# Attention scores of two heads in two 64-row halves of TensorE, straight from the summed keys, in a fused attention and MoE kernel

## Chip, cores and metric

The kernel runs on one core of one Trainium2 chip. The metric is the device time of one execution in microseconds; the time of the kernel before is the median of three runs. The profile is of one further execution, whose own time and span are in the table below.

## The reference

Attention over pooled keys and values (8 batches, 8 heads, 576 queries, head size 64; 8 neighbouring keys or values are averaged, so 72 remain), then a feed-forward layer with a fixed activation:

```python
k_p = k.reshape(B, H, Sp, pool, D).mean(axis=3)
v_p = v.reshape(B, H, Sp, pool, D).mean(axis=3)
scores = scale * np.matmul(q, k_p.transpose(0, 1, 3, 2))
scores = scores - np.max(scores, axis=-1, keepdims=True)
attn = np.exp(scores)
attn = attn / (np.sum(attn, axis=-1, keepdims=True) + 1e-09)
attn_out = np.matmul(attn, v_p)
...
h = x @ w_in
sp = np.maximum(h, 0.0) + np.log1p(np.exp(-np.abs(h)))
g = h * erf(sp)
return (g @ w_out).astype(np.float32)
```

Here x is the attention's output as 4608 rows (tokens) of 512, w_in is 512 x 2048, w_out 2048 x 512.

## The kernel before

The 4608 tokens are nine chunks of 512. Chunk 0 goes through both matrix products directly, while its weights are still being brought in and split. The other eight chunks go in four pairs, and each pair's two products are done by a Strassen scheme: seven products in place of eight, on sums of weight blocks and sums of token blocks. All long products are fp32r products of 128 x 128 weights with 512 tokens, each done three times (`three`, line 742: high limb by high limb, high by low, low by high). They make up 3120 of TensorE's products and nearly all of its time.

**Attention** (`job`, line 515). A batch's pooled keys are made first. `load_pool` (line 523) brings in one pair of heads at a time, [128 rows, 72 keys, 8 neighbours], where rows 0 to 63 are the head size of one head of the pair and rows 64 to 127 that of the other, and DVE sums the 8 neighbours into the tile `ks` (line 529). Two copies on ACT (line 543) then spread `ks` over the block-diagonal tile `kbd`, [128, pair, 2 x 72]: one head's rows in the first 72 columns, the other's in the last 72, zeros elsewhere (filled once, line 426). Values are pooled in the same way into `vs`.

Queries come in tiles of 128, and one of 64 at each batch's end: 32 tiles of 128 and 8 of 64. For a tile, `scores` (line 576) does one product per pair of heads, in fp32: all 128 rows of queries as weights, 144 columns of `kbd` as the moving side, so that both heads' scores stand beside each other. Pairs 0 and 1 go into one PSUM bank, pairs 2 and 3 into another. DVE then takes the maxima (line 588), ACT the exponentials (through Sigmoid), DVE and POOL the sums and the division; TensorE transposes the result (lines 631 and 634) and multiplies it with the values (lines 674 and 675).

**Order of the work.** Nothing waits in program order by itself: `Program` (line 129) takes every operation with an engine, a cost in ns, a priority and the buffers it holds, plays the machine through eight times, and writes out the order of the shortest play for each engine. Its inputs include the number of places of each kind of buffer (`sizes`, `CAPS`, `PLACES`) and the cost that an operation is written down with (500 ns for two score products, line 583). Where the play leaves TensorE idle in the first 57 us of the planned time, it puts filler products in (`pr.filler`, line 998: a bf16 product of constants that nobody reads, into a PSUM bank kept aside for that time), which keep TensorE's clock up.

For the first pair of chunks (s = 1), `sums` (line 484) makes the weight sums on the chip: it reads raw weights back from HBM (`raw_hbm`, tile `sw`), DVE and POOL add them (lines 495 to 498), they are split into limbs (tile `ws`) and stored. `sides` (line 699) makes the sums and limbs of the tokens. `quad` (line 811) then does the seven products of one block of w_in. `head` (line 803) does one of these seven, A11 with B11, ahead of time for the first 7 of the 8 blocks, and keeps its result in the tile `p1`.

The lines of the loops over queries, and of scores before and after, are in the listing.

Of the kernel before, what the change touches and what calls it, by code (L numbers as in the profile page):

```python
# [11 lines left out]
F32 = mybir.dt.float32  # L12
# [8 lines left out]
POOL = 8  # L21
# [26 lines left out]
ON_DVE = 8  # L48
STORE = 6
HEADS = 7  # L50
EARLY, READY = (0, 0, 20, 32, 32), 14
ON_ACT = (0,)
CAPS = {"g": 32, "x": 28, "xr": 11, "w": 14, "ws": 10, "w0": 36, "gl": 12, "t": 6, "f": 3, "q": 2, "q0": 4, "f0": 14, "v": 3, "vm": 1, "low": 2, "sw": 8,
        "h": 6, "o": 4, "att": 4, "cv": 2, "dl": 3, "p1": 8}
SLACK, SLACK_SP, BIAS = 30, 400, 2000
FILL, MARGIN = 57000.0, 300
# [3 lines left out]
PLACES = 87  # L60
# [68 lines left out]
class Program:  # L129
# [100 lines left out]
    def once(self):  # L230
# [16 lines left out]
        spare = None  # L247
        if self.filler:
            spare = heapq.heappop(slots["bank"])
            self.idle.place = spare[1]  # L250
        for _ in self.ops:
# [39 lines left out]
            if spare is not None and o.eng == "PE":  # L291
                if start > FILL:
                    heapq.heappush(slots["bank"], (start, spare[1], None))
                    spare = None
                else:
                    idle = start - max(free["PE"], 3000.0) - MARGIN - (1800 if not free["PE"] else 0)
                    out.extend([self.filler] * int(idle / 107))
# [54 lines left out]
def moe_attention(ctx: ExitStack, tc: tile.TileContext, cst, qa, kl, vl, wi, wo, out):  # L352
# [13 lines left out]
    sizes = {"u": PLACES, "bank": 8, "raw": 2, "et": 1, "etb": 1, "s": 2, "m": 2, "z": 2, "bb": 1, "ks": 1, "vs": 1, "d": 5}  # L366
# [56 lines left out]
    kbd = const.tile([P, NP, 2 * SP], F32, name="kbd")  # L423
    va = const.tile([P, NP, P], F32, name="va")
    vb = const.tile([P, NP, D], F32R, name="vb")
    nc.gpsimd.memset(kbd, 0.0)
    KBD, VA, VB = (Kept() for _ in range(3))
# [85 lines left out]
    xt, made = {}, {}  # L513

    def job(ck, b, tiles, off, times, first, fresh):

        base, due, whole = times[0], times[-1] + VAL_R, ck > 2
        if fresh:
            ks, vs = buf("ks", [NP, SP]), buf("vs", [NP + 2, D])

            on_dve = b < ON_DVE

            def load_pool(src, dst, p, size, prio, tag):
                shape = [size, POOL] if on_dve else [POOL, size]
                t = buf("raw", shape) if tag == "raw" else place("v", F32, shape)
                op("SP", 15 * size, prio - 1, lambda: nc.sync.dma_start(
                    t.ap, src.rearrange("(p a b) -> p a b", p=P, b=t.ap.shape[2])), [], [t])
                if on_dve:
                    op("DVE", dve(8 * size), prio, lambda: nc.vector.tensor_reduce(  # L529
                        dst.ap[:, p, :], t.ap, AX.X, ALU.add), [t], [(dst, p)])  # L530
                else:
                    op("POOL", gps(4 * size), prio, lambda: nc.gpsimd.tensor_add(
                        t.ap[:, 0:4], t.ap[:, 0:4], t.ap[:, 4:8]), [t], [t])
                    op("POOL", gps(2 * size), prio, lambda: nc.gpsimd.tensor_add(
                        t.ap[:, 0:2], t.ap[:, 0:2], t.ap[:, 2:4]), [t], [t])
                    op("POOL", gps(size), prio, lambda: nc.gpsimd.tensor_add(
                        dst.ap[:, p, :], t.ap[:, 0], t.ap[:, 1]), [t], [(dst, p)])

            for p in range(NP):
                load_pool(kl[b, p], ks, p, SP, base + KEYS + KEYS_R * p, "raw")  # L540
            for r0, c0 in ((64, 0), (0, SP)):
                sl = slice(r0, r0 + 64)
                op("ACT", act(4 * SP), base + KEYS_S, lambda c0=c0, sl=sl: nc.scalar.copy(
                    kbd[sl, :, c0:c0 + SP], ks.ap[sl]), [ks], [(KBD, r0)])
            for p in range(NP + 2):
                load_pool(vl[b, p], vs, p, D, base + VALS + VALS_R * p,
                          "v")
# [454 lines left out]
    for o in ops:  # L1002
        o.fn()
# [37 lines left out]
```

## Time and profile before

| what | value |
|---|---|
| median of 3 runs (lowest, highest) | 871.18 us (869.67, 877.29) |
| the profiled execution | 870.09 us |
| its span, first to last instruction | 868.3 us |
| mean granted clock of TensorE | 0.996 |
| TensorE busy | 850.9 us, 98% of the span |
| VectorE (DVE) busy | 698.6 us, 80% |
| ScalarE (ACT) busy | 574.4 us, 66% |
| GpSimd (POOL) busy | 459.9 us, 53% |
| moved by DMA | 218.04 MB, 251 GB/s on average |

How to read it: the span leaves out what lies before the first and behind the last instruction. "Busy" of TensorE counts overlapping products once, and it counts fillers. PEld is TensorE's loading of weights, which runs beside its products. A product's duration holds the tail of the array's pipeline; the distance from one start to the next is what it costs in a row of products. The granted clock is 1.00 at full speed.

### The profile page before, as it was taken

What the parts mean: (1) busy time and instruction counts of PE and PEld (TensorE: products, weight loads), DVE (VectorE), ACT (ScalarE), POOL (GpSimd) and SP (SyncE); (2) the same over time, 40 slices, a digit from 0 to 9 for tenths busy, and PEclk for the clock granted to TensorE, in tenths of its full rate; (3) what the DMA queues carried; (4) which work ended last, traced back from release to release, by engine and by line L of the source; (5) the groups of instructions that cost most, each with busy time, mean ns of one, the idle gap of its engine ahead of it and who ended that gap; (6) DMA issues with size and microseconds to landing.
All of it is one profiled execution on the core that took longest, in us unless ns stands there. A gap on an engine that the chain in (4) does not pass through costs nothing.

```text
span 868.3 us, 13644 instructions
## 1 busy us (share of the span) xinstructions
PE 850.9 (98%) x4134; PEld 702.7 (81%) x4134; DVE 698.6 (80%) x1272; ACT 574.4 (66%) x989; POOL 459.9 (53%) x482
## 2 busy tenths in 40 slices
PE   8999999799999999999999999999999999999998
PEld 7787788687888888888888888887887888888886
DVE  4987898989887888688798997877879975767872
ACT  4889877569884455478985642978866446777640
POOL 2888697567786774065557352564474323442310
PEclk9999999989999999999999999999999999999999
DMA  8899999997999899885285578924753679447541
GB/s 307 312 307 342 303 402 332 324 359 266 295 316 349 331 348 311 314 317 174 85 303 160 163 257 275 362 86 134 224 152 109 219 254 340 126 131 256 190 157 50
DMA packets 125208, 218.04 MB, mean 251 GB/s; under 512 B 16976, under 2 KB 31440, under 8 KB 125136
## 3 DMA queue, kind: packets, MB, share of 16 engines
q1 hardware_dynamic: 125136, 217.18, 72.6%
q8 instruction: 33, 0.54, 0.2%
q14 instruction: 39, 0.32, 0.1%
HBM read 167.84 MB, written 49.28 MB: 250 GB/s over the span
## 4 chain that ended last, share of the span: by engine, by line
PE 72%; DVE 2%; issue 0%; ACT 0%; DVEq 0%
PE o L746 36%; PE h L746 29%; PE att L579 3%; PE att L674 3%; PE att L631 1%; PE att L675 1%; DVE g L766 0%; DVE gl L411 0%; PE att L634 0%; DVE g L894 0%; DVE g L831 0%; DVE f L918 0%; DVE ks L529 0%; DVE t L831 0%; DVE s L624 0%
## 5 line engine op out<-in xcount | busy, mean ns | idle before, releaser
L746 PE MATMUL o<-gl,w 128*128 128x512 f32 x1584 | 377.1, 393 | 0.5 <-DVE g L769 0.3
L746 PEld LDWEIGHTS o<-gl,w 128*128 128x128 f32 x1584 | 292.7, 188 | 61.9 <-DVE gl L411 0.9
L746 PE MATMUL h<-x,w 128*128 128x512 f32 x1344 | 316.9, 392 | 2.0 <-DVE t L831 1.2
L746 PEld LDWEIGHTS h<-x,w 128*128 128x128 f32 x1344 | 249.7, 188 | 55.8 <-DVE t L831 2.5
L766 POOL TENSOR_TENSOR g<-d,g 128x512 f32<-128x512 f32 x68 | 90.7, 1351 | 98.7 <-ACT d L762 75.8
L399 ACT ACTIVATE gl<-g 128x512 fp32r<-128x512 f32 x185 | 109.3, 625 | 46.2 <-DVE g L894 20.2
L411 POOL TENSOR_TENSOR gl<-g,gl 128x512 fp32r<-128x512 f32 x67 | 100.0, 1501 | 66.8 <-ACT gl L399 32.4
L411 DVE TENSOR_TENSOR gl<-g,gl 128x512 fp32r<-128x512 f32 x149 | 110.2, 767 | 6.2 <-POOL gl L400 3.9
L831 DVE TENSOR_TENSOR g<-t,h 128x512 f32<-128x512 f32 x96 | 65.5, 684 | 31.6 <-PE h L746 29.9
L758 ACT ACT_TABLE_LOAD x48 | 61.6, 1283 | 20.7 <-PE h L746 20.0
L762 ACT ACTIVATE d<-d 128x1024 f32<-128x1024 f32 x72 | 73.7, 1054 | 0.4
L894 POOL TENSOR_TENSOR g<-g 128x512 f32<-128x512 f32 x36 | 51.8, 1439 | 25.0 <-DVE g L894 19.3
L758 ACT ACTIVATE d<-g 128x512 f32<-128x512 f32 x103 | 59.1, 623 | 5.6 <-DVE g L831 5.4
L831 DVE TENSOR_TENSOR t<-t,h 128x512 f32<-128x512 f32 x57 | 39.0, 685 | 27.8 <-PE h L746 26.1
L746 PE MATMUL h<-x,ws 128*128 128x512 f32 x192 | 48.4, 407 | 4.5 <-POOL sw L496 2.9
L762 ACT ACT_TABLE_LOAD x40 | 51.3, 1283 | 0.7
L399 ACT ACTIVATE x<-xr 128x512 fp32r<-128x512 f32 (+2 forms) x60 | 32.5, 563 | 28.9 <-DVE xr L720 21.5
L746 PEld LDWEIGHTS h<-x,ws 128*128 128x128 f32 x192 | 38.0, 199 | 13.1 <-POOL sw L496 3.0
L674 PE MATMUL att<-et,va 128*128 128x256 f32 (+3 forms) x192 | 45.5, 339 | 2.0 <-DVE s L604 1.4
L579 PE MATMUL att<-kbd,q 128*128 128x144 f32 (+1 forms) x320 | 45.9, 287 | 0.4 <-DVE x L694 0.4
L579 PEld LDWEIGHTS att<-kbd,q 128*128 128x128 f32 (+1 forms) x320 | 42.3, 179 | 5.0 <-issue 1.6
L642 ACT COPY et<-att 128x512 f32<-128x512 f32 (+1 forms) x40 | 21.8, 544 | 34.5 <-PE att L631 33.5
(91 smaller groups left out, 1145.3 us busy)
## 6 DMA issues: line engine op xcount, KB each, us to landing
w<-ws SPq DMA_DIRECT2D x192, 256.0 KB, 4.5
w<-wo SPq DMA_DIRECT2D x136, 256.0 KB, 3.6
w<-wi SPq DMA_DIRECT2D x96, 256.0 KB, 5.0
ws<-ws SPq DMA_DIRECT2D x64, 256.0 KB, 4.0
v<-vl SPq DMA_DIRECT2D x48, 256.0 KB, 5.7
raw<-kl SPq DMA_DIRECT2D x32, 288.0 KB, 4.5
out<-f SPq DMA_DIRECT2D x36, 256.0 KB, 2.0
q<-qa SPq DMA_DIRECT2D x32, 256.0 KB, 5.2
```

What stands on the lines that cost most here:

```text
L399: op("ACT", act(n), prio, lambda: nc.scalar.activation(dst(), src(), AF.Copy, scale=scale), *access, turn=turn, alt=("POOL", 0.833 * n + 1 ...
L411: both(True, dve(n), gps(n), prio + 0.1, lambda e: e.tensor_sub(lo(), src(), f32(hi())), reads + [hikey], [lokey])
L579: nc.tensor.matmul(o, raw.ap[:, p, :T], kbd[:, p], start=(p % 2 == 0), stop=True, skip_group_check=True)
L631: nc.tensor.transpose(pa.ap[:, P * p:P * p + T], sp[:, p, 0:P], ident[:T, :T])
L642: op("ACT", act(4 * T, True), r + 2.3, lambda: nc.scalar.copy(et.ap[:, :, cs], pav()), [pa], [(et, k)])
L674: nc.tensor.matmul(o, va[:, p], et.ap[:, p, :n], start=e == 0, stop=False, skip_group_check=True)
L746: nc.tensor.matmul(o, u, v, start=first and q == 0, stop=last and q == 2, skip_group_check=True)
L758: nc.scalar.activation(y(k), hs[k][0].ap, AF.Softplus)
L762: op("ACT", act(1024), prio + 0.2, lambda k=k: nc.scalar.activation(ys[k].ap, ys[k].ap, AF.Erf), own[2 * k:2 * k + 2], own[2 * k:2 * k + 2 ...
L766: both(True, dve(512), gps(512), prio + 0.3, lambda e, k=k, h=h: e.tensor_mul(h.ap, y(k), h.ap), [own[k], h], [h])
L831: op("DVE", dve(512), prio, lambda: nc.vector.tensor_add(dst.ap, u.ap, o.ap), [u, o], [dst])
L894: both(True, dve(512), gps(512), prio, lambda e: e.tensor_sub(out.ap, u.ap, v.ap), [u, v], [out])
```

## The change

1. **Scores in halves.** `kbd`, its fill and its copies are gone. For each pair of heads, two products now take the place of one: the queries' rows 64 to 127 with the 72 keys of `ks` in the same rows, and rows 0 to 63 with theirs. Each is placed in its own half of the array's rows (`tile_position`), and each half writes a PSUM bank of its own. One operation issues all eight products of a tile, in every chunk. Banks hold heads by parity now, so maxima, differences and exponentials address heads in steps of two.
2. **Keys' places.** Keys come in with 64 keys of one pair at a time (the size of the values' tiles, so that both use the common places, kind "k", at most 5) and one transfer with the last 8 keys of all four pairs. `ks` and `bb` are double-buffered; `s`, `m` and `z` have four buffers.
3. **Score buffers.** PSUM banks for attention ("att") are at most 6 where they were 4; places are 89 where they were 87.
4. **A12 products.** `neck` does the product of A12 with B21 ahead of time for the first 4 blocks of s = 1, and adds it to `p1` at once.
5. **Fillers** go into the bank that the next product is about to use, not into one kept aside, and stand also behind 57 us of the planned time where the plan idles TensorE for over 1.2 us.

```diff
-HEADS = 7
+HEADS, NECKS = 7, 4
...
-FILL, MARGIN = 57000.0, 300
+FILL, MARGIN, LONG_IDLE = 57000.0, 300, 1200.0
...
-PLACES = 87
+PLACES = 89
...
+            if o.eng == "PE":
+                new = [b for b in o.bufs if b.home == "bank" and not b.held]
+                idle = start - max(free["PE"], 3000.0) - (1800 if not free["PE"] else 0)
+                if new and (start < FILL or idle > LONG_IDLE):
+                    begin = max(free["PE"], 4800.0 if not free["PE"] else 0.0, slots["bank"][0][0])
+                    out.extend([(self.filler, new[0])] * int((start - begin - MARGIN) / 107))
...
-            for r0, c0 in ((64, 0), (0, SP)):
-                sl = slice(r0, r0 + 64)
-                op("ACT", act(4 * SP), base + KEYS_S, lambda c0=c0, sl=sl: nc.scalar.copy(
-                    kbd[sl, :, c0:c0 + SP], ks.ap[sl]), [ks], [(KBD, r0)])
...
+            for p in range(NP):
+                load_pool(kl[b, n * p:n * p + n], lambda p=p: ks.ap[:, p, :D], (ks, p),
+                          base + KEYS + KEYS_R * p, "k", (D,))
+            load_pool(kl[b, n * NP:], lambda: ks.ap[:, :, D:], (ks, NP), base + KEYS + KEYS_R * NP, "k", (NP, SP - D))
...
-            def scores(ps):
-                for p in ps:
-                    o = pss[p // 2].ap[:T, 2 * SP * (p % 2):2 * SP * (p % 2) + 2 * SP]
-                    nc.tensor.matmul(o, raw.ap[:, p, :T], kbd[:, p], start=(p % 2 == 0), stop=True,
-                                     skip_group_check=True)
-
-            for g in (range(2),) if whole else ((0,), (1,)):
-                op("PE", 500 * len(g), r, lambda g=g: scores([2 * i + e for i in g for e in range(2)]),
-                   [raw, KBD], [pss[i] for i in g], [s, m, z], turn="q")
+            def scores():
+                for p in range(NP):
+                    for x in range(2):
+                        half = slice(D * (1 - x), D * (2 - x))
+                        nc.tensor.matmul(pss[x].ap[:T, SP * p:SP * p + SP], raw.ap[half, p, :T], ks.ap[half, p],
+                                         start=p == 0, stop=True, skip_group_check=True, tile_position=(D * (1 - x), 0))
+
+            op("PE", 4 * 130, r, scores, [raw, ks], pss, [s, m, z], turn="q")
...
+    def neck(s, i, x, due, p1):
+
+        a12 = piece(lambda: in_hbm[i][:, 1], IN[i], due)
+        A, g = bank("h"), place("g")
+        product(A, a12, "B21", x, due, False, True)
+        op("DVE", dve(512), due + 0.3, lambda: nc.vector.tensor_add(g.ap, p1.ap, A.ap), [p1, A], [g])
+        return g
```

The planner writes out a new order. Three places of it follow. In the rows, a product's name is output<-inputs, then partitions x elements of the output, and xN counts like instructions in a row; an fp32 or fp32r product's weight load is part of its row.

On TensorE, behind the input products of the first pair of chunks (o: output products, att: the attention's banks). Before:

```order
L746 MATMUL h<-x,ws 128x512 x6
L746 MATMUL o<-gl,w 128x512 x6
L579 MATMUL att<-kbd,q 128x144 x4
L746 MATMUL o<-gl,w 128x512 x12
L579 MATMUL att<-kbd,q 64x144 x4
L746 MATMUL o<-gl,w 128x512 x60
```

Now:

```order
L731 MATMUL h<-x,ws 128x512 x6
L565 MATMUL att<-ks,q 128x72 x8
L731 MATMUL o<-gl,w 128x512 x12
L565 MATMUL att<-ks,q 64x72 x8
L731 MATMUL o<-gl,w 128x512 x24
```

A tile's four products of 144 columns are eight of 72, and each block of them still stands between long products.

On TensorE, ahead of the first product with summed weights (ws), where chunk 0 ends. Before:

```order
L746 MATMUL h<-x,w 128x512 x12
L674 MATMUL att<-et,va 128x128
L675 MATMUL att<-etb,vb 64x128
...
L746 MATMUL h<-x,ws 128x512 x18
L746 MATMUL h<-x,w 128x512 x12
L746 MATMUL h<-x,ws 128x512 x24
```

Now (the last two rows ahead of ws are one filler; there are 36):

```order
L731 MATMUL h<-x,w 128x512 x24
L659 MATMUL att<-et,va 128x128
L660 MATMUL att<-etb,vb 64x128
L991 LDWEIGHTS cst
L991 MATMUL h<-cst 128x256
...
L731 MATMUL h<-x,ws 128x512 x18
L731 MATMUL h<-x,w 128x512 x6
L731 MATMUL h<-x,ws 128x512 x24
```

The 24 products of the four `neck`s stand ahead of ws, fillers behind them, and the first four blocks have 6 products with plain weights between those with sums where they had 12. In all there are 208 fillers now and 206 before; 145 of them stand ahead of the first long product, where all 206 stood.

On SyncE, the first transfers of keys, queries, values and input weights (d: raw input weights). Before:

```order
L526 DMA raw<-kl 128x576 x2
L571 DMA q_215<-qa 128x512
L571 DMA q_217<-qa 128x512
L526 DMA v<-vl 128x512
L526 DMA raw<-kl 128x576 x2
L526 DMA v<-vl 128x512
```

Now:

```order
L520 DMA k<-kl 128x512 x3
L556 DMA q_216<-qa 128x512
L520 DMA k<-kl 128x512
L520 DMA k<-kl 128x256
L556 DMA q_223<-qa 128x512
L520 DMA v<-vl 128x512 x2
```

All keys of the first batch come ahead of its values. Further on, the fourth and fifth transfers of input weights, which stood ahead of the third batch's keys, stand behind the first two of these and one more transfer of queries.

More of the change, by code (lines that the diff above doesn't have):

```diff
@@ L365, in moe_attention @@
     hbm = pool("hbm", 1, space=bass.MemoryType.DRAM)
-    sizes = {"u": PLACES, "bank": 8, "raw": 2, "et": 1, "etb": 1, "s": 2, "m": 2, "z": 2, "bb": 1, "ks": 1, "vs": 1, "d": 5}
+    sizes = {"u": PLACES, "bank": 8, "et": 1, "etb": 1, "s": 4, "m": 4, "z": 4, "bb": 2, "ks": 2, "vs": 1, "d": 5}
     sizes.update(CAPS)
@@ L421, in moe_attention @@
     nc.scalar.activation(warm, warm, AF.Sigmoid)
-    kbd = const.tile([P, NP, 2 * SP], F32, name="kbd")
     va = const.tile([P, NP, P], F32, name="va")
     vb = const.tile([P, NP, D], F32R, name="vb")
-    nc.gpsimd.memset(kbd, 0.0)
-    KBD, VA, VB = (Kept() for _ in range(3))
+    VA, VB = (Kept() for _ in range(2))
     in_hbm = [hbm.tile([P, 2, 2, 256], F32R, tag=f"wi{ft}", name=f"wi{ft}") for ft in range(NJ)]
@@ L518, in job @@
         if fresh:
[L519 to L537, printed above, removed]
@@ L819, in quad @@
         s2, s3, s1 = sm(1), sm(2), sm(0)
-        a12 = piece(lambda: in_hbm[i][:, 1], IN[i], due)
+        if g00 is None:
+            a12 = piece(lambda: in_hbm[i][:, 1], IN[i], due)
         a22 = piece(lambda: in_hbm[i + NQ][:, 1], IN[i + NQ], due)
         s4 = sm(3)
-        A, Bk, C, Dk = (bank("h") for _ in range(4))
+        A, Bk, C, Dk = (None if m == 0 and g00 else bank("h") for m in range(4))
         n = [0]
@@ L834, in quad @@
         fts = (i, i + NQ)
-        g = {(m, t): place("g") for m in range(2) for t in range(2)}
+        g = {(m, t): g00 if g00 and m + t == 0 else place("g") for m in range(2) for t in range(2)}
         if not early:
@@ L845, in quad @@
         add(g[1, 1], u, Dk, due + 1.0)
-        if early:
+        if early and not g00:
             next(A, a12, "B21", False, True)
@@ L980, in moe_attention @@
         ps = [head(s, i, x, start(s) - 1) for i in range(HEADS if s == 1 else 0)]
+        g00s = [neck(s, i, x, start(s) - 0.5, ps[i]) for i in range(NECKS if s == 1 else 0)]
         for i in range(NQ):
-            quad(s, i, x, start(s), ps[i] if i < len(ps) else None)
+            quad(s, i, x, start(s), ps[i] if i < len(ps) else None, g00s[i] if i < len(g00s) else None)
         span = SHORT if s < NC // 2 else 16
@@ L993, in moe_attention @@
             seconds(s, start(s) + LONG, span)
-    idle = bank("h")
     cb = c.bitcast(mybir.dt.bfloat16)
-    pr.idle = idle
-    pr.filler = Op("PE", 107, 0, lambda: nc.tensor.matmul(
-        idle.ap[:, :256], cb[:, :P], cb[:, :256], start=True, stop=True))
+    pr.filler = lambda b: nc.tensor.matmul(b.ap[:, :256], cb[:, :P], cb[:, :256], start=True, stop=True)
     ops = pr.order()
-    small.tile([P, 272], F32, tag="pad", name="pad")
+    small.tile([P, 208], F32, tag="pad", name="pad")
     for o in ops:
-        o.fn()
+        if isinstance(o, tuple):
+            o[0](o[1])
+        else:
+            o.fn()
 def kernel(q, k, v, moe_w_in, moe_w_out):
```

59 lines of the change are left out of this document (30 added, 29 removed).

## Prediction

> **What bounds the kernel now.** I read the page's busy times first, then the busy times by stage, then the timeline of TensorE around single score blocks, and last the waits.
>
> ```profile
> span 868.3 us, 13644 instructions
> PE 850.9 (98%) x4134; PEld 702.7 (81%) x4134; DVE 698.6 (80%) x1272; ACT 574.4 (66%) x989; POOL 459.9 (53%) x482
> ```
>
> TensorE is busy for 98% of the span, but in the start part of that is filler products. The stages tell where a saved microsecond of TensorE counts (columns: stretch, its length, busy time of PE, PEld, DVE, ACT and POOL with instruction counts, granted clock, DMA share, GB/s):
>
> ```profile
> 10.00:44.50 34.50, 32.08 (x258) 26.90 (x256) 29.32 (x71) 26.45 (x104) 22.52 (x30) 1.00 0.92 334
> 57.00:160.00 103.00, 100.57 (x506) 82.92 (x506) 85.90 (x168) 84.37 (x150) 81.32 (x96) 1.00 0.99 345
> 168.00:170.70 2.70, 0.07 (x1) 0.10 (x1) 2.70 (x6) 1.03 (x6) 1.62 (x3) 1.00 1.03 291
> 170.70:172.80 2.10, 0.48 (x2) 0.17 (x2) 2.10 (x8) 1.85 (x5) 1.00 (x1) 0.79 1.05 405
> 172.80:178.80 6.00, 6.00 (x14) 4.71 (x15) 4.54 (x16) 1.23 (x4) 3.35 (x1) 0.50 1.02 336
> 178.80:225.00 46.20, 45.01 (x196) 36.26 (x194) 43.40 (x66) 41.90 (x50) 33.40 (x43) 1.00 0.90 311
> 225.00:863.80 638.80, 638.57 (x3026) 529.06 (x3027) 506.97 (x902) 401.57 (x647) 301.85 (x288) 1.00 0.66 226
> ```
>
> From 225 us to the end TensorE idles 0.23 us of 638.80: what a score block gains or loses there moves the end one for one. Up to 160 us the DMA engines are the second bound (share 0.92 to 0.99). Around 170 us TensorE stands still, and then runs at a granted clock of 0.50 for 6 us.
>
> **The score blocks: what one costs.** Each record of an fp32 score product is one of two passes, and a query tile has 4 products, so 8 records: 32 tiles of 128 queries, 8 of 64.
>
> ```profile
> L579 PE MATMUL att<-kbd,q 128*128 128x144 f32 x256 | 36.4, 286 | 0.0
> L579 PE MATMUL att<-kbd,q 128*64 128x144 f32 x64 | 9.6, 292 | 0.4 <-DVE x L694 0.4
> ```
>
> A duration of 286 ns has the tail of the pipeline in it; the price is read from the chain and from the timeline. In the chain, long products take 75.50/333 = 0.227 us, and a 128-query block 0.98 us, 0.1225 a pass:
>
> ```profile
> 247.07 0.98 PE att L579 x8
> 788.24 75.50 PE o L746 x333
> ```
>
> Now three pieces of TensorE's timeline: a 128-query block, a 64-query block (it uses 64 of the array's columns), and the transposes of a 64-query tile (they use 64 of its rows).
>
> ```profile
> 120.62 0.62 PE L746 MATMUL o<-gl,w 128*128 128x512 f32 x2
> 121.08 1.14 PE L579 MATMUL att<-kbd,q 128*128 128x144 f32 x8
> 121.96 0.95 PE L746 MATMUL o<-gl,w 128*128 128x512 f32 x3
> ...
> 106.88 0.61 PE L746 MATMUL o<-gl,w 128*128 128x512 f32 x2
> 107.42 1.19 PE L579 MATMUL att<-kbd,q 128*64 128x144 f32 x8
> 108.54 0.96 PE L746 MATMUL o<-gl,w 128*128 128x512 f32 x3
> ...
> 605.69 0.61 PE L746 MATMUL h<-x,w 128*128 128x512 f32 x2
> 606.24 0.46 PE L631 MATMUL att<-cst,s 64*128 64x64 f32 x4
> 606.54 0.22 PE L634 MATMUL att<-cst,bb 64*64 64x64 f32 x1
> 606.68 0.96 PE L746 MATMUL h<-x,w 128*128 128x512 f32 x3
> ```
>
> The first piece lasts 121.96+0.95-120.62 = 2.29 us. It holds five long products (5x0.23), the last one's tail (0.39-0.23 = 0.16) and 0.98: 2.29, nothing over. The second lasts 2.62 with the same contents: 0.33 over. The third lasts 1.95; its five short products go one every 0.06 (below), 1.15+0.16+0.31 = 1.62: again 0.33 over. So **going into a part of the array and back costs 0.33 us**, and every score block of the changed kernel works in 64-row halves. The 8 short blocks pay it already (0.98+0.33 = 1.31); the 32 full ones would pay it anew.
>
> What a pass takes is the larger of its stream and its weight load. The stream of 144 keys took 0.1225, so 72 take about 0.0625. The load hides behind the stream now; how long it is shows where streams are short, in the rows of PE's weight loads:
>
> ```profile
> 92.68 0.30 PEld L674 LDWEIGHTS att<-et,va 128*128 128x128 f32 x2 [1.49 <-issue]
> 92.89 0.14 PEld L675 LDWEIGHTS att<-etb,vb 96*64 96x64 f32 x1
> ...
> 606.24 0.32 PEld L631 LDWEIGHTS att<-cst,s 64*128 64x128 f32 x4 [0.35 <-issue]
> 606.48 0.11 PEld L634 LDWEIGHTS att<-cst,bb 64*64 64x64 f32 x1
> ```
>
> Two loads of 128 columns on all rows take 92.89-92.68 = 0.21, or 0.105 each, against 0.0625 of stream: **after the change the load is the longer one**. Transposes load 64 rows in 0.24/4 = 0.06, but they are another kind of product, so I take 0.105 and keep 0.06 as a bound. The tile now has 16 loads where it had 8. No row shows two halves at work at once, so the block is bounded from both sides:
> - loads of the two halves side by side, 0.105 each: eight steps 0.84, the last stream 0.06, the switch 0.33, and 0.05 because the first load lies open (128 columns, not the 64 of the row above): 1.28. A full block loses 0.30, a short one (loads under 0.0625: 0.50+0.06+0.33 = 0.89) gains 0.42. Sum: 32x0.30-8x0.42 = +6.2 us.
> - loads one after another: 16x0.105+0.33+0.05 = 2.06, +1.08 a full block; short 16x0.0625+0.33 = 1.33, +0.02. Sum +34.7.
> - side by side, loads at 0.06: 0.89 for both kinds, 32x(-0.09)-8x0.42 = -6.3.
>
> I take the first: halves are separate rows, and the stream's rate, the load's rate and the switch are rows of this trace. The Trainium skill (TensorE: Matmul & The Clock Gate, LDWEIGHTS (loading the stationary operand)) says that a load takes as long on few rows as on all, columns over 1.2 GHz, 0.107 us for 128; the 0.105 agrees for full rows, none here shows 64, and by it the third case falls away. The same page (Part 3: Packing small matmuls) lets a load for another row group be pulled ahead of products in flight; no run here shows it, and by it the sum is the first.
>
> **The order of the work.** Three terms. *Start*: all 206 fillers stood before the first long product, 145 do now; each takes (4.20-0.27)/36 = 0.109 us. The copies into kbd (0.87) leave the first tile's path:
>
> ```profile
> 14.05 4.20 PE L998 MATMUL h<-cst 128*128 128x256 bf16 x37
> ...
> 10.95 0.87 ACT L543 COPY kbd<-ks 64x288 f32<-64x288 f32 x2 [8.72 <-DVE ks L529]
> ```
>
> 61x0.109 = 6.6 us earlier at most, nothing at least: the input weights then come later on SP's queue, behind more keys and queries, and the DMA engines have no slack until 160 us. I take -2. *The stall near 170 us*: lost now are 2.63+1.62 idle and half of the 6.00 at clock 0.50, 7.25 us. Who was late:
>
> ```profile
> PE h L746 <- POOL sw L496: 2.9, 1, 2.9
> PE h L746 <- DVE x L411: 1.6, 1, 1.6
> 171.80 4.35 POOL L495 TENSOR_TENSOR sw<-sw 128x256 f32<-128x256 f32 x1 [2.10 <-DMA sw<-wf]
> ```
>
> The summed weights and the limbs of x come no sooner. But 24 products (four A12, 5.5 us) now stand ahead, and 36 fillers (3.9 us) that keep the clock up: bounds -7.25 and 0; I take 7.25-3.9, -3.3. *What is late next*: four of the quads behind the stall have 30 products where they had 36, and DVE, busy 43.40 of 46.20 us there, must bring the same sums in less time: 0 to +5.5 (all that moved ahead given back); +2.
>
> Work that I cost at nothing: ACT loses 16 copies of 0.43 us, POOL a fill of 0.58, both with a third or more of the span free; DVE's 32 key sums of 0.741 become 32 like the values' 0.672 and 8 small ones, about 0.4 by the difference of the two per element (1.08 ns): +1.4 us, hidden while DVE stays at 80%, and worth 1.4 if all of it met the start. In the first three chunks a maximum now waits for the whole block and not for its own bank, half a block (0.5) later; that falls among fillers or long products, and costs at most 1 in the start's chain.
>
> ```profile
> L529 DVE TENSOR_REDUCE vs<-v 128x64 f32<-128x512 f32 x48 | 31.7, 672 | 6.0 <-DMA v<-vl 5.9
> L529 DVE TENSOR_REDUCE ks<-raw 128x72 f32<-128x576 f32 x32 | 23.3, 741 | 5.9 <-DMA raw<-kl 5.8
> L543 ACT COPY kbd<-ks 64x288 f32<-64x288 f32 x16 | 6.9, 430 | 12.4 <-DVE ks L529 8.7 <-PE att L579 3.4
> L426 POOL MEMSET kbd<- 128x576 f32 x1 | 0.6, 579 | 0.0
> ```
>
> Sum: +6.2-2-3.3+2 = +2.9, so a span of 868.3+2.9 = 871.2. The profiled execution took 870.09, 1.8 around its span; the median of the runs is 871.18. I forecast 871.18+2.9 = **874 us**. With the order's bounds this case reaches from 863 (-6.6, -7.25, 0) to 885 (0, 0, +5.5, +1.4, +1 for shared banks).
>
> **Rivals.**
> 1. *Loads one after another* (slower): the load of the other half waits until the product before it has started, as each load does in the rows now; it decides once 16 loads of 0.105 outlast 8 passes of 0.1225. 34.7-6.2 = 28.5 more, less 2 because a slower TensorE gives the other engines time: 900. For it: in the trace loads never lie side by side. Against it: they never had different rows.
> 2. *Loads of half the rows are short* (0.06, as in the transposes): 12.5 less than forecast, 861.
> 3. *Halves at full profit and no switch*: a block is 8x0.0625+0.06 = 0.56, 32x0.42+8x0.75 = 19.4 saved; with the order's terms, and 2 more given back to late sums, 874-25.6+2 = 850. Against it: 0.33 over in both kinds of partial blocks. The Trainium skill (TensorEngine Tiling (Array Packing), Theoretical Speedup) gives up to twice the rate for a contraction of 64 or less; by it the full block would be 0.49; no run here shows it.
> 4. *The halves don't run at once at all*, streams in turn at 0.0625: as rival 1 in full blocks (the loads bind there), so it has no time of its own.
>
> **How the numbers follow.** Forecast case 0.42, rival 1 0.24, rival 2 0.20, rival 3 0.12, anything else 0.02. About 1% (8.7 us) is what a measurement tells from no change. Faster by more (under 862.5): all of rival 3, 0.11 of rival 2, 0.07 of the forecast case: 0.30. Slower by more (over 879.9): rival 1, 0.07 of the forecast case and the rest: 0.33. Within: 0.37. The range for 8 of 10 leaves out about a tenth on each side: 854 to 902; the forecast case's own is 863 to 885.
>
> **What would show it.** In the timeline, from the start of a 128-query block's first product to the next long one's second: 1.28 plus one long product is the forecast, 2.06 rival 1, 0.9 rivals 2 and 3. Loads of 128 columns 0.105 apart in pairs, or one at a time, tells 1 from the forecast; a wait ahead of each block's first load of some 0.1 us more than 0.23 is the switch. Near 170 us the clock should stay at 1.00. The first long product should start some microseconds before 44.5 and then wait for weights. The forecast is wrong if full blocks come out at or under 0.98, or if TensorE idles more than 8 us behind 225 us.

## The result, and the profile after

| kernel | median us | ratio to before (95% interval) | profiled execution | its span |
|---|---|---|---|---|
| before | 870.78 (15 runs) | | 870.09 | 868.3 |
| the change | 866.68 (15 runs, 865.21 to 868.3) | 0.9936 [0.992, 0.9953] | 868.08 | 866.3 |

The forecast was 874, 2.9 us more than before; measured are 4.1 us less in medians. The ratio speaks for 5.6 us (its interval for 4.1 to 7.0): the runs of before spread upwards, to 877.46. The two profiled executions differ by 2.0 us only: that of before was 0.7 under the median of these runs, that of the change 1.4 over its own (it has a stretch of 3.4 us at half clock near 80 us). What follows is compared with the 2.0 where it comes from the traces.

The page of the change:

```profile
span 866.3 us, 14281 instructions
PE 851.8 (98%) x4456; PEld 697.3 (80%) x4456; DVE 698.4 (81%) x1284; ACT 567.6 (66%) x975; POOL 452.5 (52%) x473
```

TensorE is busy for 0.9 us longer in a span 2.0 us shorter. The stages, in the columns of the prediction:

```profile
57.00:160.00 103.00, 99.07 (x549) 79.42 (x548) 88.59 (x171) 82.35 (x152) 80.05 (x92) 0.98 1.01 359
168.00:170.70 2.70, 2.70 (x13) 2.23 (x13) 2.19 (x5) 0.58 (x2) 0.62 (x2) 1.00 0.97 369
170.70:172.80 2.10, 2.10 (x19) 1.82 (x18) 1.60 (x6) 0.83 (x2) 1.70 (x3) 1.00 1.18 360
172.80:178.80 6.00, 6.00 (x41) 5.16 (x40) 4.77 (x16) 3.65 (x8) 2.50 (x3) 1.00 0.97 334
178.80:225.00 46.20, 43.82 (x191) 35.30 (x190) 38.12 (x55) 40.98 (x49) 40.69 (x50) 1.00 0.95 327
225.00:862.00 637.00, 637.00 (x3244) 524.13 (x3243) 508.14 (x913) 392.01 (x630) 292.21 (x278) 1.00 0.66 223
```

Near 170 us nothing stands still and the clock stays at 1.00, though 36 fillers (3.9 us) are part of that busy time; behind it TensorE now idles 2.38 us of 46.20, where it idled 1.19. Up to 160 us it idles 3.93 us of 103, where it idled 2.43.

**One score block.** TensorE's timeline of the change: a 128-query block, a 64-query block, and two blocks in one visit between long products.

```profile
243.15 1.07 PE L731 MATMUL h<-x,ws 128*128 128x512 f32 x4
244.15 1.11 PE L565 MATMUL att<-ks,q 64*128 64x72 f32 x16
245.19 1.19 PE L731 MATMUL o<-gl,w 128*128 128x512 f32 x4
...
247.14 1.07 PE L731 MATMUL o<-gl,w 128*128 128x512 f32 x4
248.14 0.72 PE L565 MATMUL att<-ks,q 64*64 64x72 f32 x16
248.79 1.45 PE L731 MATMUL o<-gl,w 128*128 128x512 f32 x5
...
273.83 0.84 PE L731 MATMUL o<-gl,w 128*128 128x512 f32 x3
274.61 1.76 PE L565 MATMUL att<-ks,q 64*64 64x72 f32 x32
276.30 1.66 PE L731 MATMUL o<-gl,w 128*128 128x512 f32 x6
```

From the start of the last long product ahead to the start of the second one behind, less two long products (0.460), a full block takes 1.242 us where it took 0.98, a short one 0.846 where it took 1.319. The single records say why. The 16 of a full block start in pairs, 7 ns between the two halves and then 105: 0.112 a pair, where a pass of before took 0.1225; in a short block a pair takes 0.063. The second pair comes 0.055 later than this pace, which fits a first load that lies open. The switch shows against a full block of before, which has none. From the last long product to the first score product it is 0.318 where it was 0.228: 0.09 on the way in. The first long product comes 0.20 behind the last score product where it came 0.028 behind: 0.17 on the way out. The second one follows 0.338 after the first, but it did so in before as well (0.335), so that this step is no part of the switch. So the pairs save some 0.07 us a full block (seven steps of 0.1225 less 0.112), and the switch with the open load costs 0.32. Two blocks in one visit (what TensorE does between two long products) share this: a short and a full one together take 1.886, apart 2.088; two full ones 2.135, apart 2.484.

Where the time came from is told by milestones. This table is worked out from the traces, not a view of them: the start (us) of the k-th of the 3120 long products, in the two kernels and in some of the experiments below.

```
k                     0     120     240     360     480     720    3119
before             44.5    72.9   108.5   146.8   187.7   244.2   864.0
the change         37.3    64.6   103.1   146.3   182.3   240.0   862.1
b_halves           45.9    73.7   106.2   146.2   186.0   242.5   864.5
a_kbd              36.7    64.0   104.4   149.0   183.8   239.7   861.3
a_keys             36.6    65.8   100.3   141.1   184.1   244.3   865.0
b_necks_fill       44.0    72.2   107.8   146.9   185.3   239.7   866.0
b_slack27          43.3    70.6   103.9   146.6   186.5   243.3   863.2
a_slack27          36.3    64.8   101.5   147.5   182.7   239.9   861.3
b_slack            46.0    74.9   105.4   146.6   187.7   242.1   863.5
a_slack33          37.0    64.3   105.1   144.7   184.5   240.0   861.8
b_nf_slack         45.7    73.5   104.5   145.2   183.1   237.6   859.7
```

The change starts its long products 7.2 us earlier, has 0.5 of that left at the 360th, gains 4.9 between the 360th and the 480th (the stall), gives back 1.2 by the 720th and 2.3 in the stretch from there that TensorE bounds.

### The profile page after: what moved, and what is told of

Read it like the earlier page. It is cut to its first block, busy times and chain, and to the rows that moved or that the text cites. A ratio compares the mean times of both kernels' runs of the same rounds, so it can differ in the third digit from the quotient of the medians.

```text
span 866.3 us, 14281 instructions
## 1 busy us (share of the span) xinstructions
PE 851.8 (98%) x4456; PEld 697.3 (80%) x4456; DVE 698.4 (81%) x1284; ACT 567.6 (66%) x975; POOL 452.5 (52%) x473
## 4 chain that ended last, share of the span: by engine, by line
PE 85%; DVE 4%; POOL 4%; DMA 3%; issue 2%; SPq 1%; ACT 0%; POOLq 0%
PE o L731 40%; PE h L731 33%; PE att L565 4%; PE att L659 3%; PE att L616 2%; DMA wi<-w 1%; POOL w L405 1%; POOL low L446 1%; PE att L660 1%; PE att L991 1%; SPq L463 1%; DMA k<-kl 1%; DVE ks L523 1%; DMA sw<-wf 1%; DVE f L450 1%
## 5 line engine op out<-in xcount | busy, mean ns | idle before, releaser
L405 POOL TENSOR_TENSOR gl<-g,gl 128x512 fp32r<-128x512 f32 x71 | 111.7, 1584 | 57.9 <-ACT gl L393 29.8
L393 ACT ACTIVATE gl<-g 128x512 fp32r<-128x512 f32 x187 | 108.8, 622 | 47.0 <-DVE g L888 15.1
L405 DVE TENSOR_TENSOR gl<-g,gl 128x512 fp32r<-128x512 f32 x145 | 108.0, 770 | 4.7 <-ACT gl L393 2.9
L888 POOL TENSOR_TENSOR g<-g 128x512 f32<-128x512 f32 x33 | 45.9, 1394 | 22.7 <-DVE g L888 20.7
L605 POOL TENSOR_TENSOR bb<-s,z 128x64 f32<-128x64 f32 (+1 forms) x40 | 15.2, 382 | 74.1 <-DVE z L599 56.4
L888 DVE TENSOR_TENSOR g<-g 128x512 f32<-128x512 f32 x63 | 46.2, 740 | 0.9
L393 ACT ACTIVATE x<-xr 128x512 fp32r<-128x512 f32 (+2 forms) x54 | 29.1, 562 | 27.1 <-DVE xr L705 22.2
L731 PE MATMUL h<-x,ws 128*128 128x512 f32 x192 | 45.4, 390 | 0.9 <-DVE g L825 0.9
L565 PEld LDWEIGHTS att<-ks,q 64*128 64x128 f32 (+1 forms) x640 | 36.5, 176 | 10.8 <-issue 6.8
L573 DVE TENSOR_REDUCE m<-att 128x4 f32<-128x288 f32 (+1 forms) x80 | 33.8, 449 | 11.3 <-PE att L565 10.8
```

The source lines that it names most:

```text
L393: op("ACT", act(n), prio, lambda: nc.scalar.activation(dst(), src(), AF.Copy, scale=scale), *access, turn=turn, alt=("POOL", 0.833 * n + 1 ...
L405: both(True, dve(n), gps(n), prio + 0.1, lambda e: e.tensor_sub(lo(), src(), f32(hi())), reads + [hikey], [lokey])
L565: nc.tensor.matmul(pss[x].ap[:T, SP * p:SP * p + SP], raw.ap[half, p, :T], ks.ap[half, p], start=p == 0, stop=True, skip_group_check=True, ...
L573: op("DVE", dve(4 * SP), r + 0.4, lambda pv=pv, g=g: nc.vector.tensor_reduce(mx()[:, :, g], pv(), AX.X, ALU.max), [ps], [(m, g)])
L731: nc.tensor.matmul(o, u, v, start=first and q == 0, stop=last and q == 2, skip_group_check=True)
L888: both(True, dve(512), gps(512), prio, lambda e: e.tensor_sub(out.ap, u.ap, v.ap), [u, v], [out])
```

## The experiments

Eighteen runs. Those named a_ start from the change, those named b_ from the kernel before. "Told" is the cost in ns that the planner is given for a block of scores, which only sets its order.

### The change taken apart

**b_halves**: the kernel before with the halves alone (two `ks`, no `kbd`), the planner told the 1000 it was told before.

```diff
-op("PE", 500 * len(g), ...scores([2 * i + e ...]), [raw, KBD], [pss[i] for i in g], ...)
+op("PE", 1000, r, scores, [raw, ks], pss, [s, m, z], turn="q")   # eight products in halves
```

> The kernel before with the scores in halves alone: keys straight from the sums (two buffers of them), no block-diagonal tile; planner's cost of a tile's scores left at 1000 ns, keys' and score buffers, fillers and A12 products as before. Theory A (the halves cost TensorE +0.26 us a full block and -0.47 a short one, +4.6 in all; the gain of the change is the order's): slower than before by 3 to 6 us, about 875. Theory B (the halves bring the gain, since keys need no copies and the start moves up): faster than before by 2 to 4 us, about 867.

Measured: 870.99, 0.9999 [0.9974, 1.0025], span 868.7. Neither case. Its stages:

```profile
57.00:160.00 103.00, 102.64 (x568) 83.34 (x567) 87.71 (x174) 84.47 (x146) 74.72 (x91) 1.00 0.96 328
225.00:864.00 639.00, 638.42 (x3232) 522.97 (x3231) 508.48 (x904) 403.16 (x638) 292.13 (x285) 1.00 0.67 227
```

It pays for the blocks where TensorE bounds: from the 720th long product to the last 622.1 us, before 619.8. It has that back from the stages ahead, where it idles 0.36 us of 103 instead of 2.43 and is 1.7 us ahead at the 720th product. From 44.5 to 165 us TensorE has three waits in before, none of them for a copy into `kbd`, and here one of 0.3 us. Those of before:

```profile
PE att L674 <- DVE s L604: 1.4, 1, 1.4
PE h L746 <- DVE g L769: 0.8, 1, 0.8
PE o L746 <- DVE g L769: 0.3, 1, 0.3
```

**a_kbd**: the change with block-diagonal scores (`kbd`, its copies and its fill) for all tiles, one place less for the room that `kbd` takes; told 520, as the change.

```diff
+nc.tensor.matmul(o, raw.ap[:, p, :T], kbd[:, p], start=(p % 2 == 0), stop=True, ...)
-PLACES = 89
+PLACES = 88
```

> The changed kernel with the scores taken back: block-diagonal keys, copies on ACT, products of 144 columns, no halves; everything else as changed (A12 products, fillers, keys' loads, buffers), the planner told the same 520 ns a tile, one place fewer to make room. Theory A: 4.6 us less than the changed kernel, about 862. Theory B: the lead of the start is lost and the time goes back to 869 or more.

Measured: 866.31, 0.9934 [0.9908, 0.996], span 865.5: the change without its halves takes as long as with them. TensorE idles 6.62 us of 57 to 160 here, against the change's 3.93, and it is 2.7 us behind the change at the 360th long product. But it is level at the 720th (239.7 and 240.0), and takes 621.6 us from there, with 8 late fillers (0.9 us), where the change takes 622.1 with 19 (2.1): what the halves cost late doesn't show between these two orders. The early stretch:

```profile
57.00:160.00 103.00, 96.38 (x484) 78.41 (x483) 89.61 (x175) 80.34 (x148) 81.15 (x95) 0.98 0.89 304
```

**a_keys**: the change without halves, `neck`s and late fillers; the keys' places, score buffers and fillers' banks stay, one place less as in a_kbd. Told 1000.

```diff
-HEADS, NECKS = 7, 4
+HEADS, NECKS = 7, 0
-FILL, MARGIN, LONG_IDLE = 57000.0, 300, 1200.0
+FILL, MARGIN, LONG_IDLE = 57000.0, 300, 1e9
```

> The changed kernel without halves (block-diagonal keys, planner told 1000 ns), without the early A12 products and without fillers behind 57 us of the plan: what is left of the change is the keys' loads, the score buffers and the places. If these and the earlier start are the gain: 866 to 868. If the stall at 170 us comes back with its half clock: 869 to 872, with the first long product at about 37 us all the same and its lead gone at 160 us.

Measured: 871.32, 1.0003 [0.9988, 1.0018], span 869.2. It is 7.9 us ahead at the first long product, 5.7 at the 360th and nothing at the 720th. Its stages and the first of TensorE's waits (us in total, times, longest):

```profile
160.00:168.00 8.00, 3.94 (x23) 3.08 (x21) 7.88 (x23) 5.87 (x19) 1.97 (x3) 0.95 0.88 331
168.00:180.00 12.00, 9.85 (x35) 7.99 (x36) 9.87 (x27) 5.44 (x13) 3.22 (x5) 0.75 1.01 356
```

```profile
PE h L750 <- DVE t L844: 3.7, 1, 3.7
PE att L638 <- POOL bb L624: 3.3, 2, 3.0
PE h L750 <- ACT x L393: 3.2, 1, 3.2
PE h L750 <- DVE x L405: 3.0, 1, 3.0
```

An earlier start only arrives earlier at the limbs of x: the waits of 3.2 and 3.0 us for them (L393, L405) are the 6.2 us idle from 160 to 180, with 6.8 us of half clock. The 3.7 us stand near 220 us, at sums of a quad, and half clock follows there too (3.4 us).

**b_necks_fill**: the kernel before with the change's items 4 and 5 (`neck` and the new rule for fillers; 240 fillers, 212 of them ahead of the first long product, where the expectation says 181).

```diff
+HEADS, NECKS = 7, 4
+FILL, MARGIN, LONG_IDLE = 57000.0, 300, 1200.0
```

> The kernel before with the four early A12 products and the new rule for fillers (no bank kept aside, fillers also late), and its own scores, keys' loads, buffers and places: 181 fillers ahead of the first long product and 25 more than 57 us into the plan. If the stall at 170 us was what the change gains: 4 to 5 us less than before, 866. If it is the keys' places and buffers with the earlier start: within 2 us of before, 869 to 871.

Measured: 872.1, 1.0015 [1.0003, 1.0027], span 870.2. The stall closes, as it does in the change, and the kernel is 4.5 us ahead at the 720th product. But 6.5 are lost behind it, most of it from 475 to 520 us, where TensorE idles 3.3 us, 1.97 of it for a late limb of POOL, and 3.4 us of half clock follow:

```profile
160.00:180.00 20.00, 20.00 (x110) 16.74 (x110) 17.50 (x42) 13.18 (x34) 9.18 (x14) 1.00 0.85 300
475.00:520.00 45.00, 41.69 (x192) 33.96 (x191) 39.18 (x65) 24.36 (x47) 28.12 (x15) 0.96 0.51 172
```

```profile
510.51 5.07 PE L741 MATMUL o<-gl,w 128*128 128x512 f32 x14 [1.97 <-POOL gl L406]
```

**a_nonecks** and **a_nolongidle**: the change without `neck`s, and the change without the fillers behind 57 us of the plan.

```diff
-HEADS, NECKS = 7, 4
+HEADS, NECKS = 7, 0
```

> The changed kernel without the four early A12 products. If they are what fills the stall at 170 us: 2 to 5 us slower than the changed kernel, 869 to 871, with more fillers or idle time there. If the fillers alone do it by keeping the clock up (or the products only move the work): within 1 us of it, 866 to 868.

```diff
-FILL, MARGIN, LONG_IDLE = 57000.0, 300, 1200.0
+FILL, MARGIN, LONG_IDLE = 57000.0, 300, 1e9
```

> The changed kernel without fillers behind 57 us of the planned time: 153 of the 208 stay; the 36 ahead of the first summed weights, the 19 at 284 us and nothing else go, the order is the same. Theory A: the 19 are a pure loss in a stretch that TensorE bounds (2.2 us back), the 36 fill a wait that is there anyhow, but without them the clock falls to half for 3.4 to 6.8 us, 1.7 to 3.4 lost: together 865.5 to 868. Rival (the clock does not matter, fillers only cost): 864 or less.

Measured: 868.04, 0.996 [0.9939, 0.9981], and 866.24, 0.9946 [0.9924, 0.9967]. Without `neck`s the plan puts 90 fillers into the wait, the clock holds, and the kernel stays within 1.4 us of the change. Without late fillers 145 are left (the expectation says 153), the clock drops to half twice (3.4 us at 88, 3.4 at 187), and nothing is lost in sum: 19 of the late fillers stand in the stretch that TensorE bounds. By the starts there they take 2.1 us, and from the 720th product to the last a_nolongidle is 1.5 us shorter than the change. The timeline of the change there:

```profile
282.98 1.11 PE L565 MATMUL att<-ks,q 64*128 64x72 f32 x16
284.03 2.25 PE L991 MATMUL att<-cst 128*128 128x256 bf16 x19
286.11 0.60 PE L616 MATMUL att<-cst,s 128*128 128x128 f32 x4
```

### What a pass costs

**a_wide**: the change with 108 columns streamed per product, where 72 are needed.

```diff
-nc.tensor.matmul(pss[x].ap[:T, SP * p:SP * p + SP], raw.ap[half, p, :T], ks.ap[half, p],
+c0 = min(SP * p, NP * SP - 108)
+nc.tensor.matmul(pss[x].ap[:T, 108 * p:108 * p + 108], raw.ap[half, p, :T],
+                 ks.ap[half].rearrange("p a k -> p (a k)")[:, c0:c0 + 108],
```

> The changed kernel with 108 columns streamed in each score product instead of 72 (the further columns are other pairs' keys, so the scores are wrong ones). A pass streams 0.0925 us and not 0.0625. If weight loads bind a full block (0.105 a load, the two halves' side by side): its starts still come in pairs 0.112 apart, block longer by at most 0.04. If streams bind it, the block is 0.24 longer (side by side) or 0.48 (in turn). Short blocks, whose loads take half, must be longer by 8 x 0.03 = 0.24 in either case.

Measured: 867.54 in one run, span 865.8. A full and a short block in its timeline:

```profile
114.32 0.84 PE L733 MATMUL o<-gl,w 128*128 128x512 f32 x3
115.09 1.15 PE L566 MATMUL att<-ks,q 64*128 64x108 f32 x16
116.16 1.19 PE L733 MATMUL o<-gl,w 128*128 128x512 f32 x4
...
244.81 0.84 PE L733 MATMUL o<-gl,w 128*128 128x512 f32 x3
245.58 0.96 PE L566 MATMUL att<-ks,q 64*64 64x108 f32 x16
246.47 0.74 PE L733 MATMUL o<-gl,w 128*128 128x512 f32 x2
```

Half as much stream again costs a full block 0.03 us (its pairs stay 0.112 apart) and a short block 0.24 (0.063 becomes 0.093). The load of 128 columns sets the full block's pace, the stream the short one's.

### Where a microsecond of TensorE counts

**a_early** and **a_late**: the change with four filler products ahead of each score block, in the first 13 tiles (5.7 us in all) or in the other 27 (11.8 us). The plan is not told.

```diff
+for _ in range(4 if ck <= 2 else 0):      # a_late: ck > 2
+    nc.tensor.matmul(pss[0].ap[:, :256], cb[:, :P], cb[:, :256], start=True, stop=True)
```

> The changed kernel in the same order, with four fillers (0.44 us) more in each score block of the first 13 tiles, those that stand ahead of 225 us: 5.7 us of TensorE work. Theory D (a block's price counts only where TensorE bounds, behind 225 us; ahead of it the extra falls into waits that are there anyhow): 0 to 2.5 us slower than the changed kernel. Rival (each block's price counts, as the forecast summed it): 5 to 6.5 us slower.

> The same four fillers in each score block of the other 27 tiles: 11.8 us of TensorE work. Theory D: all of it shows, 11 to 12.5 us slower than the changed kernel. Rival (the later stretch has slack too): under 9.

Measured: 870.34, 0.9999 [0.9984, 1.0013], 3.7 above the change; and 879.08, 1.0088 [1.0059, 1.0117], 12.4 above it. Late, everything counts, as its row says (no idle time in 635 us); early, two thirds do, between the two expectations.

```profile
225.00:860.00 635.00, 635.00 (x3286) 520.63 (x3286) 502.44 (x905) 390.43 (x627) 288.81 (x277) 1.00 0.66 222
```

### The planner's prices

**b_cheap**: before, told 520 a tile where it was told 1000. **a_honest**: the change, told near what the traces show, 1230 and 835, where it is told 520. **a_mix**: the change, with block-diagonal scores for full tiles and halves for short ones, told 980 and 835.

```diff
+op("PE", 260 * len(g), r, ...)                                       # b_cheap
+op("PE", 1230 if T == P else 835, r, scores, ...)                    # a_honest
+wide_tile = T == P                                                   # a_mix: kbd for these
+op("PE", 980, r, whole_scores, ...)  /  op("PE", 835, r, scores, ...)
```

> The kernel before, with only the planner told that a tile's scores cost 520 ns and not 1000; no instruction is added but fillers, the order differs. Theory C (the change's gain is what any other plan may bring): 3 us or more off 870.7 either way. Theory A: within 2 us of it.

> The changed kernel with the planner told what a tile's scores take on the chip, 1230 and 835 ns in place of 520. Theory A: the late fillers stand only where TensorE does wait, so the 2.2 us at 284 us come back and nothing else changes much: 863 to 866. Theory C: any value from 862 to 871.

> The changed kernel with halves for the 8 short tiles only; the 32 full tiles use the block-diagonal keys; planner told 980 and 835 ns; one place fewer. Theory A: the full blocks give back 32 x 0.26 = 8.4 us and the short ones keep their gain, so 858 to 861, the least of all. Theory B: 866 to 869, since the copies are back in the start.

Measured: 873.35, 1.0036 [1.0023, 1.0049]; 861.51, 0.9897 [0.9877, 0.9916]; 862.08, 0.9883 [0.9849, 0.9917]. a_honest is a kernel of the same arithmetic as the change, in another order, and 5.2 us faster, more than the change itself gains in medians; it lies just under its cases, a_mix 1.1 us above its lower one. a_mix is as far ahead at the 360th long product (143.6 us, a_honest 143.2, the change 146.3), and takes 618.7 us from the 720th product to the last (9 late fillers, 1.0, among them) where a_kbd takes 621.6 (8, 0.9): 3.0 less without these fillers, which is about the 6 short blocks' gain (6 x 0.473 = 2.8); but orders of before alone differ by 1.5 us in this stretch (619.8, 619.9, 621.3).

### How much of this is the chance of an order

When the planner chooses the next operation, it adds SLACK times the priority to the earliest start; SLACK is 30 in both kernels. At 27 or 33 it writes other orders of the same work, with other fillers.

```diff
-SLACK, SLACK_SP, BIAS = 30, 400, 2000
+SLACK, SLACK_SP, BIAS = 33, 400, 2000     # b_slack27, a_slack27: 27
```

> The kernel before with one constant of the planner's order changed (SLACK 30 to 33) and no work added or removed beyond fillers (233). A, the chance of the order is small: within 1.5 us of the kernel before, 869.3 to 872.3. C, the chance is as large as the differences told so far: more than 2.5 us away from it on either side, as b_cheap's 2.6 above.

> The kernel before with the necks and the new rule for fillers, as in b_necks_fill (872.1), but with SLACK 33 in the planner. A, the gain of about 4.5 us at the stall near 170 us is real and the later stall of b_necks_fill was chance of its order: 866 to 868. C, each order of it makes its own stall: 870 or more. The stall near 170 us closes in both cases, so that the 720th long product starts 3 to 5 us earlier than in b_slack.

> The change with the planner told 1230 and 835 ns for the two shapes of score block, as in a_honest (861.5), but with SLACK 33. A, true prices make the better order: 860 to 864. C, 861.5 was a lucky order: 866 or more, about the change's own 866.7.

> The kernel before with the planner's constant SLACK at 27 in place of 30, a third order of the same work. If the chance of the order is 3 us or so, as b_slack says: anywhere from 866 to 874. If the order before was an unlucky one among its like: 866 to 869, as b_slack.

> The change with SLACK at 27. C, the change's gain is the chance of two orders: not below b_slack27 by more than 1.5 us, or above it. D, the change is worth some 4 us whatever the order: 3 to 6 us below b_slack27.

> The change with SLACK at 33, beside b_slack (868.2, 0.9965). C, the gain is the chance of two orders: 867 or more. D, the change is worth some 4 us whatever the order: 862 to 865.

Medians and ratios to before; each row has one piece of work, each column one SLACK:

| | 27 | 30 | 33 |
|---|---|---|---|
| before | 869.47, 0.9971 [0.995, 0.9992] | 870.78 | 868.22, 0.9965 [0.9944, 0.9986] (b_slack) |
| the change | 866.15, 0.9939 [0.9915, 0.9962] | 866.68, 0.9936 [0.992, 0.9953] | 867.72, 0.9962 [0.9945, 0.9979] |
| change less before, us | -3.3 | -4.1 | -0.5 |
| before with `neck`s and fillers | | 872.1, 1.0015 [1.0003, 1.0027] | 868.26, 0.9952 [0.9928, 0.9975] (b_nf_slack) |
| the change, told 1230 and 835 | | 861.51, 0.9897 [0.9877, 0.9916] | 866.03, 0.9932 [0.9908, 0.9956] |

A constant that means nothing for the work moves a kernel by up to 4.5 us in medians. So the pair at 33 speaks for chance, the pair at 27 for a gain of 3 to 6 us. Over the three the gain is 2.6 us in medians and 2.9 by the ratios (2.8, 5.6 and 0.3); at 33 the two intervals lie almost on each other, and that pair shows no difference. The profiled executions agree better among themselves (spans of 868.3, 867.4 and 867.8 before, 866.3, 865.8 and 866.0 after, 1.6 to 2.0 less each time), but each is one execution out of a spread: that of b_slack is the slowest of its ten runs, 1.5 us over their median, that of a_slack33 lies on its median, those of the change and of a_slack27 are 1.4 over theirs. Their agreement is no better evidence than the medians. b_nf_slack closes the stall again (4.5 us ahead of b_slack at the 720th product) without the later stall of b_necks_fill, which thus belonged to one order; in its profiled execution (span 864.0) 3.8 of it are left at the end, but its median is that of b_slack, so no gain is shown for that part alone. Of a_honest's 5.2 us under the change, 1.7 are left at SLACK 33, where the intervals overlap, and 866.03 is the case of a lucky order: whether a true price makes the better order is not shown.

The stall differs most from order to order. TensorE in a_slack33:

```profile
169.95 0.38 PE L659 MATMUL att<-et,va 128*128 128x128 f32 x2
170.08 0.30 PE L660 MATMUL att<-etb,vb 96*64 96x128 f32 x1
170.23 7.60 PE L991 MATMUL h<-cst 128*128 128x256 bf16 x68
177.59 4.37 PE L731 MATMUL h<-x,ws 128*128 128x512 f32 x18
```

and in the change:

```profile
171.24 0.38 PE L659 MATMUL att<-et,va 128*128 128x128 f32 x2
171.38 0.30 PE L660 MATMUL att<-etb,vb 96*64 96x128 f32 x1
171.52 4.10 PE L991 MATMUL h<-cst 128*128 128x256 bf16 x36
175.38 2.99 PE L731 MATMUL h<-x,ws 128*128 128x512 f32 x12
```

Both rows read as a busy TensorE at full clock, but fillers are time in which the products with `ws` do not run: 68 of them last 7.4 us, 36 of them 3.9. In both, attention's last products ahead of the wait end at the same time within 1.3 us; a_slack33 has won only the clock, the change also some of the wait.

## Why the prediction was wrong, point by point

The time lies inside the stated range, 854 to 902, but it moved the other way than forecast. Its terms against what three pairs of orders show, one profiled execution each. The forecast's +6.2 for scores is split at the 13th tile, after which 21 full and 6 short tiles are left (21x0.30-6x0.42 = +3.8), so that 11x0.30-2x0.42 = +2.5 stand ahead. Differences of the milestones, change less before, at SLACK 27, 30 and 33:

| stretch | forecast | measured (27, 30, 33) | mean |
|---|---|---|---|
| up to the 360th long product: start, first tiles' scores | -2+2.5 = +0.5 | +0.9, -0.5, -1.9 | -0.5 |
| 360th to 480th: the stall | -3.3 | -4.7, -4.9, -1.3 | -3.6 |
| 480th to 720th: late sums | +2 | +0.4, +1.2, +1.1 | +0.9 |
| 720th to the last: scores where TensorE bounds | +3.8 | +1.5, +2.3, +0.5 | +1.4 |
| sum | +2.9 | -1.9, -1.9, -1.6 | -1.8 |

- **The step that failed** is the sum "32x0.30-8x0.42 = +6.2 us". Its unit prices were nearly right (0.262 and 0.473), and so was each mechanism: loads side by side at 0.105 with a_wide showing that they bind the full block, the switch of a third of a microsecond (0.32 with the open load), and none of the four rivals came true. What was wrong is the multiplication: every one of 40 blocks at full price. Measured, the halves alone are worth nothing, and with 0 in place of 6.2 the forecast's own sum gives 871.18-2-3.3+2 = 867.9, 1.2 us over the change.
  - Where TensorE bounds, the measured prices make 21x0.262-6x0.473 = +2.7. All visits between long products in that stretch, from the starts of the products around them and less one long product each, take 68.0 us before, 69.7 in the change without its 19 fillers, 70.1 in a_slack27, 69.7 in a_slack33 and 70.5 in b_halves: +1.7 to +2.5. The change has three double visits there, before one, and each shares one switch (0.20 to 0.35). The change also has fewer visits there, 58 for 69, and the first step from long product to long product behind a visit is some 0.08 us longer than the others, with or without halves: 1.0 us less. So its +2.3 are +1.8 for visits, +2.1 for late fillers, -1.0 for visits that it doesn't make, and half a microsecond spread over the rest.
  - In the first 13 tiles TensorE waits for others as well, so a block's microsecond counts for two thirds (a_early), and it waits less there with the halves: idle time from 57 to 160 us went from 2.43 to 0.36 when they were put into the kernel before, and was 3.93 with them where it was 6.62 without, in the change's setting. I had costed the 16 copies into `kbd` that vanish at nothing ("both with a third or more of the span free"). The trace of before doesn't show that it was these: the waits of TensorE that went are for DVE (1.4 us for the scores less their maximum, 1.1 for `g`, L769), none for `kbd`. What took them away was not separated from the new order that each kernel gets.
  - The halves by themselves thus made no difference: 0.9999 [0.9974, 1.0025] in one setting, which leaves some 2 us either way, and a_kbd against the change (866.31 and 866.68) in the other; each in one order only.
- **The load's price.** The Trainium skill (TensorE: Matmul & The Clock Gate, LDWEIGHTS (loading the stationary operand)) has a load on few rows last as long as one on all, 0.107 us for 128 columns; the pairs 0.112 apart agree, and rival 2 fell with it. The Trainium skill (TensorEngine Tiling (Array Packing), Theoretical Speedup) gives up to twice the rate for a contraction of 64 or less, an estimate of 0.49 us for a full block at best. Measured are 1.242: the load sets the pace there, and the switch comes on top; in a short block a pair at 0.063 is twice the rate of a pass at 0.1225, and with the switch the block takes 0.846.
- **The start.** The first long product starts 7.2 us earlier, at the bound of 6.6 and a little over; of it 0.5 is left at the 360th product, and in a_keys none of the lead passes the stall. The term of -2 stood for what remains; it was too large, in these pairs, by about the spread of the orders.
- **The stall.** -3.3 against -4.7, -4.9 and -1.3: the mechanism (24 products ahead of the wait, fillers for the rest) as told, and b_necks_fill and b_nf_slack close it without the rest of the change. But a closed stall alone did not shorten the medians of these two (872.1 against 870.78, 868.26 against 868.22).
- **Late sums.** +2 against +0.4 to +1.2: right in sign and place, TensorE's idle time from 178.8 to 225 us doubling from 1.19 to 2.38. The bound of +1.4 for the keys' sums is +1.0 by the means of its rows (32x0.672+8x0.4-32x0.741); it stands only in the 885.
- **Overlooked:** that 19 of the change's fillers stand at 284 us. I told them as 208 in all with 36 at the stall, and did not ask where the others were. They take 2.1 us where every microsecond counts; neither a_slack27 nor a_slack33 has such fillers.
- **The order as a rival.** I priced edits as if the order around them stayed. An order is worth up to 4.5 us either way here, more than the sum that I forecast, and the change's 4.1 us in medians lies on its lucky side: 2.6 is the mean of three pairs. That the planner is told 520 for a block that takes 1242 was in the diff (`4 * 130`); b_cheap and a_honest show that another price moves the time as much as the edit does, by the order that it brings.

**Open:** what brings the change's gain. No part alone shows it (halves 0.9999, keys' places and score buffers 1.0003, `neck`s with the new fillers 1.0015), all but the halves does (a_kbd, 0.9934), so that an earlier start and a closed stall may be needed together, or an order that suits; and what took away the early waits that are missing with the halves.

## What to carry to other kernels

Two row halves of TensorE ran at once, but what a contraction split that way wins must pay for the switch: here it lost 0.26 us with 128 columns to load, where the load and not the stream set the pace, and won 0.47 with 64, where the stream did and a switch was paid before as well. Blocks that share a visit share the switch. Multiply a unit price only by the places where the engine bounds, and look for every filler that a rule adds outside the place it is meant for. Where a planner writes the order, run each kernel in two or three orders (a neutral constant is enough) before a gain of half a per cent is put down to the edit.

## What the runs showed of the hardware

Products and weight loads in the two row halves start 7 ns apart and run beside each other, which no row of before could show; pairs then follow at 0.112 us with 128 columns to load (0.112 also with 108 columns streamed) and at 0.063 with 64. The switch shows most of its cost on the way out, in the first long product behind the block (0.20 us after the last score product, 0.216 behind a short block of before, 0.028 behind a full one, which has no switch) and 0.09 on the way in; the second long product comes 0.325 to 0.341 after the first in all of them. The half clock behind a wait comes in pieces of 3.4 us (one or two of them), and one such piece, between 80 and 130 us, stands in 8 of the 13 kernels profiled that have the change's early start and in none of the others. It is not in a_early, which has 52 more fillers among the first tiles, but neither in a_late and a_wide, whose early order is the change's own: it comes with an execution, and that fillers keep it away is not shown.
